# A gated mix of memory attention and a ReGLU block: an earlier half of wk, a split first K, and a new written-out order

## The chip, the cores and the metric

The kernel runs on one core of a Trainium2 chip. The metric is device time in microseconds (us) of one execution; the time of a kernel is the median of its runs. Engines are named as the profile names them: PE is the matrix engine (PEld its weight loads), DVE the vector engine, ACT the scalar engine, POOL the GpSimd engine, and SP the engine that issues nearly all DMAs (SPq is its queue).

## The reference

The input x has 2048 tokens of 512 numbers, in bfloat16. Two branches read it, and a gate per token mixes them:

```
g = sigmoid(sum(x * gate_w))            # one number per token
a = attention(x, wq, wk, wv, beta) @ wo # 32 heads of 16, 4 segments of 512 tokens
b = (relu(x @ W_gate) * (x @ W_up)) @ W_down    # 1792 wide
out = g * a + (1 - g) * b
```

Within a segment s the attention is

```
p     = softmax(q k^T * scale + causal mask);  a_dot = p @ v
a_mem = phi(q) @ M / (phi(q) @ z + 1e-6)       # memory of the earlier segments
o     = sigmoid(beta) * a_mem + (1 - sigmoid(beta)) * a_dot
M += phi(k)^T @ v;  z += sum(phi(k))           # phi(t) = t + 1 if t > 0, else exp(t)
```

## The kernel before, in words

**Tiling.** The 512 input columns are four chunks of 128 (the contraction), and the 512 columns of Q and K four blocks of 128, eight heads each. A unit is one block of one segment; there are 16. The transposed input of a segment is `xT`, 128 x 4 x 512. Q and K come out transposed, each block in one PSUM bank, summed over the four chunks (L478, a full 128 x 128 matmul of 512 columns). DVE copies Q into `QT` (L569) and K into `ktr` (L585), then writes it three times into `KT` (L588) with every second head zeroed by `mcol_e` or `mcol_o`, so that one matmul of 32 rows serves one head.

**A score visit** (L636, and L649 for the diagonal pieces) is a group of row-tiled matmuls, four at a time side by side, that fills PSUM banks 0 to 3 with scores. ACT takes the exponential of all four banks in one instruction (L658) into one of six buffers `E`, or into `Em`. There are 72 visits: four for each unit and one more for every second unit. Because each visit uses banks 0 to 3, it must wait for the exponential of the visit before. POOL then clears what the causal mask forbids (L687, two instructions for each visit that goes to `E`); for `Em` DVE does it (L669).

**Output product.** `pv` (L709) multiplies E with V in two groups of column-tiled matmuls, each into a bank. DVE transposes both banks into `T` (L740), takes the reciprocal of the softmax sum (L748), multiplies it by `grc`, the gates (L750), scales (L745), and transposes back into `oT` (L721).

**Head gates.** sigmoid(beta) is computed once: ACT's exponential (L410), `head_gates` on DVE, then `row_gates` (L402, L404) spreads it into `gcat`, 20 copies on DVE, and `pair_gates` (L408) makes `bdg` of it. `grc` is the product of `gcat` and the token gate `rq`, which POOL spreads in segment 0 (L448).

**The wide block** has 14 column blocks: gate, ReLU on ACT (L873), up, product on DVE (L879) into one of 14 buffers `hT`. The output rows then sum over the 14 `hT` with `wd_sb` and over `oT` with `wo_sb`. All of these matmuls, the projections and the output rows are called flexible: they may be issued as one full matmul (L478) or as four quarters of 32 columns of weights (L482), which is the tiling of `pv`. Between two visits the matmuls form a stretch. In the kernel before, a flexible matmul is quartered if the column-tiled group `pv` stands before it in the stretch.

**What sets the order.** Every piece of work is a task of a `Plan`: an engine, a duration that the planner assumed, dependencies, and buffer slots. The planner itself is not in the file; its result is: `ORDER` lists the tasks in the order of issue, and `UNITS` the slot of each ring (which PSUM bank, which `hT`). Each engine runs its tasks in this order, and waits by semaphores where the data need it. `LANDS` are the arrival times that the planner assumed for the loads; they set nothing at run time.

**The loads at the start.** SP issues, in order: the first half of the columns of x for half of the tokens, chunk 0 of wq, the transposed second half of x (L304, chunks 2 and 3 of `xT`), chunks 2 and 3 of wq (L306), both halves of wk, wv, and the pieces of W_gate and W_up; ACT's queue issues the other half of x's first columns and chunk 1 of wq. Chunks 0 and 1 of `xT` are made by PE (L515: eight transposes) and copied by DVE and ACT (L530). Before that PE runs seven matmuls on constants (L924). In the order before, PE then does Q's chunks 0 and 1 for all four blocks, Q's chunks 2 and 3, K of three blocks, some of V, and the first score visit.

Of the kernel before, what the change touches and what calls it, by code (L numbers as in the profile page):

```python
# [12 lines left out]
P = 128  # L13
# [13 lines left out]
RQ = 5  # L27
RH = 14

ORDER = """  # L30
# [99 lines left out]
class Plan:  # L130

    def __init__(self):
        self.tasks, self.free = [], {}
# [9 lines left out]
    def add(self, *a, **k):  # L143
        t = Task(*a, **k)
        t.n = len(self.tasks)
        self.tasks.append(t)
        return t
# [32 lines left out]
def kernel(  # L180
# [492 lines left out]
    def attention(seg, c):  # L673
# [17 lines left out]
        if c % 2 == 0:  # L691
            diag(seg, c)
# [298 lines left out]
```

## Time and profile before

| what | before |
|---|---|
| median of 3 runs | 263.82 us (263.33 to 264.11) |
| span of the profiled execution | 261.6 us |
| its own time | not listed beside the span |
| PE busy | 254.8 us, 97% |
| DVE busy | 203.4 us, 78% |
| ACT busy | 183.3 us, 70% |
| POOL busy | 64.2 us, 25% |
| mean granted PE clock | 0.998 |

The span is the time from the first to the last instruction of the profiled execution; the 2.2 us up to the median lie around it. Busy times overlap between the engines. A PE row of the timeline gives its start and how long its matmuls were in flight; the ends are modelled and overlap the next row, so the pace of PE is read from the distance of two starts.

### The profile page before, as it was taken

Reading aid. Unit: us, or ns where it says so; the run is one execution under the profiler, and the core shown is the slowest. Engines: PE = TensorE matmul, PEld = TensorE weight load, DVE = VectorE, ACT = ScalarE, POOL = GpSimd, SP = SyncE. Lnnn points to the kernel's source line nnn. Section 1 sums busy time; section 2 is a strip of 40 time slices with the busy share of each in tenths; the row PEclk is TensorE's granted clock in tenths of the full one; section 3 lists DMA queues with packets and bytes.
Section 4 is the critical chain, followed back from the end, with each engine's and each line's share of the span. In section 5 each row is a group of like instructions: output and inputs, shape, how many; then the busy total and the mean of one; then the engine's idle time right before and its main releaser. Section 6 shows DMA issues by size and latency. Waiting matters only on the chain.

```text
span 261.6 us, 8758 instructions
## 1 busy us (share of the span) xinstructions
PE 254.8 (97%) x3769; PEld 117.2 (45%) x3798; DVE 203.4 (78%) x472; ACT 183.3 (70%) x168; POOL 64.2 (25%) x168
## 2 busy tenths in 40 slices
PE   8999999999999999999999999999999999999995
PEld 3444444454444454544444444445444344445454
DVE  2799999889896766948989868858988678788622
ACT  3199998998877788787768576878486768972000
POOL 8023462313322223322112222122122232120000
PEclk9999999999999999999999999999999999999999
DMA  7999885021311202100210500140200100230011
GB/s 193 305 289 283 214 262 109 4 43 23 84 34 43 89 25 80 36 0 3 84 21 3 95 4 26 58 142 3 80 4 23 32 5 23 98 107 3 3 43 40
DMA packets 31565, 19.71 MB, mean 75 GB/s; under 512 B 16040, under 2 KB 29992, under 8 KB 31528
## 3 DMA queue, kind: packets, MB, share of 16 engines
q1 hardware_dynamic: 31112, 18.90, 26.3%
q8 instruction: 29, 0.48, 0.8%
q10 hardware_dynamic: 416, 0.26, 0.3%
q14 instruction: 8, 0.07, 0.1%
HBM read 13.21 MB, written 2.55 MB: 60 GB/s over the span
## 4 chain that ended last, share of the span: by engine, by line
PE 90%; DVE 5%; DMA 1%; issue 1%; SPq 1%; ACT 0%; DVEq 0%; ACTq 0%
PE ps L478 54%; PE ps L482 19%; PE ps L636 8%; PE ps L709 7%; DMA wq_sb<-in_A_wq_dram 1%; PE ps L649 1%; DVE ktr L585 1%; DVE KT L588 1%; PE ps L829 1%; SPq L304 1%; DVE QT L569 0%; PE ps L765 0%; DVE T L740 0%; DVE hT L879 0%; PE ps L805 0%
## 5 line engine op out<-in xcount | busy, mean ns | idle before, releaser
L658 ACT ACTIVATE E<-ps 128x2048 bf16<-128x2048 f32 x64 | 120.1, 1877 | 32.0 <-PE ps L636 21.8
L687 POOL TENSOR_SCALAR_AFFINE_SELECT E<-E 128x256 bf16<-128x256 bf16 x128 | 55.6, 458 | 170.0 <-ACT E L658 169.9
L879 DVE TENSOR_TENSOR hT<-ps,rgr 128x512 bf16<-128x512 f32 x56 | 37.8, 684 | 13.1 <-PE ps L478 8.4
L478 PE MATMUL ps<-xT,wu_sb 128*128 128x512 bf16 x163 | 45.6, 380 | 0.7 <-issue 0.5
L873 ACT ACTIVATE rgr<-ps 128x512 bf16<-128x512 f32 x56 | 32.6, 596 | 15.3 <-PE ps L482 8.2
L478 PE MATMUL ps<-wd_sb,hT 128*128 128x512 bf16 (+1 forms) x174 | 41.7, 354 | 0.6 <-issue 0.5
L478 PE MATMUL ps<-xT,wg_sb 128*128 128x512 bf16 x149 | 40.9, 380 | 0.3
L740 DVE STREAM_TRANSPOSE T<-ps 128x512 f32<-128x512 f32 x32 | 22.2, 706 | 6.8 <-PE ps L709 6.6
L636 PE MATMUL ps<-QT,KT 32*128 32x320 bf16 (+3 forms) x512 | 25.4, 273 | 0.3
L478 PEld LDWEIGHTS <-wu_sb 128*128 128x128 bf16 x170 | 15.3, 98 | 19.4 <-issue 3.0
L478 PEld LDWEIGHTS <-hT 128*128 128x128 bf16 x178 | 15.6, 98 | 17.6 <-issue 2.1
L905 DVE TENSOR_SCALAR osr<-ps,ngcol 128x512 bf16<-128x512 f32 (+2 forms) x18 | 12.3, 691 | 13.3 <-PE ps L482 9.1
L478 PEld LDWEIGHTS <-wg_sb 128*128 128x128 bf16 x156 | 14.3, 98 | 17.8 <-issue 2.1
L709 PE MATMUL ps<-E,Vp 128*17 128x320 bf16 (+3 forms) x512 | 19.3, 273 | 0.0
L636 PEld LDWEIGHTS <-KT 32*128 32x128 bf16 x512 | 7.6, 92 | 25.7 <-issue 24.6
L658 ACT ACTIVATE Em<-ps 128x2048 bf16<-128x2048 f32 x8 | 15.0, 1874 | 5.0 <-PE ps L649 5.0
L482 PE MATMUL ps<-xT,wg_sb 128*32 128x512 bf16 x272 | 17.8, 379 | 0.0
L482 PE MATMUL ps<-wd_sb,hT 128*32 128x512 bf16 (+1 forms) x296 | 16.9, 359 | 0.0
L478 PE MATMUL ps<-wv_sb,xT 128*128 128x512 bf16 x59 | 16.7, 380 | 0.2
L478 PE MATMUL ps<-xT,wq_sb 128*128 128x512 bf16 x57 | 15.9, 382 | 0.5 <-DMA wq_sb<-in_A_wq_dram 0.4
L478 PE MATMUL ps<-xT,wk_sb 128*128 128x512 bf16 x54 | 15.3, 379 | 0.2 <-issue 0.2
L482 PE MATMUL ps<-xT,wu_sb 128*32 128x512 bf16 x216 | 15.0, 379 | 0.0
(100 smaller groups left out, 293.7 us busy)
## 6 DMA issues: line engine op xcount, KB each, us to landing
out_dram<-osr SPq DMA_DIRECT2D x15, 128.0 KB
wd_sb<-in_B_W_down_dram SPq DMA_DIRECT2D x2, 896.0 KB
xn<-in_A_x_dram SPq DMA_DIRECT2D x3, 512.0 KB
cdr<-coefs SPq DMA_DIRECT2D x6, 256.0 KB
xn<-coefs SPq DMA_DIRECT2D x6, 256.0 KB
wg_sb<-in_B_W_gate_dram SPq DMA_DIRECT2D x2, 512.0 KB
wu_sb<-in_B_W_up_dram SPq DMA_DIRECT2D x2, 512.0 KB
wg_sb<-in_B_W_gate_dram SPq DMA_DIRECT2D x2, 384.0 KB
```

The lines of the kernel that those rows point to most:

```text
L304: nc.sync.dma_start_transpose(out=xT[0][:, NC // 2:NC, :], in_=x[0:L, halves[1]])
L478: nc.tensor.matmul(out, lhsT=lhsT, rhs=rhs, start=start, stop=stop)
L482: nc.tensor.matmul(out[r], lhsT=lhsT[:, r], rhs=rhs, start=start, stop=stop, tile_position=(0, 32 * j))
L585: d = plan.add("DVE", 600, key - RQK, lambda: nc.vector.tensor_copy(ktr[ks.i][:], bank(sl)), [a], DVL + 40, need=[ks], frees=[sl])
L636: nc.tensor.matmul(ps[:, j * L + o:j * L + o + L - q], lhsT=KT[i][rows, kb, 3 * r:3 * r + 2].rearrange("p h q -> p (h q)"), rhs=QT[i][rows ...
L658: last_exp[0] = [plan.add("ACT", 66 + 4 * L / 1.2, key, lambda: nc.scalar.activation(dst, ps[:, 0:4 * L], ACT.Exp, scale=SCALE), [a] + war ...
L687: nc.gpsimd.affine_select(out=m[:, :, o:o + HP], in_=m[:, :, o:o + HP], compare_op=ALU.is_ge, fill=0.0, base=HP, pattern=[[0, 4], [1, HP]] ...
L709: nc.tensor.matmul(bank(sl)[32 * m:32 * m + HW, q:q + w], lhsT=(Vp[i] if n < 4 else Vm)[:, kb, r, 4 * c + j, 0:HW], rhs=rhs, start=(n == 0 ...
L740: done.append(plan.add("DVE", 633, key - RL, lambda r=r, sl=sl: nc.vector.transpose(T[ts.i][:, r], bank(sl)), [a] + done, 75 if r else 0, ...
L873: r = plan.add("ACT", 478, key - RL, lambda sl=gsl, rs=rs: nc.scalar.activation(rgr[rs.i][:], bank(sl), ACT.Relu), [g], ACL, frees=[gsl])
L879: nc.vector.tensor_tensor(hT[hs1.i][:], bank(sl), rgr[rs.i][:], ALU.mult)),
L905: nc.vector.tensor_scalar(osr[os.i][:, n0 - c0:n1 - c0], bank(sl)[:, 0:n1 - n0], ngcol[:, tt:tt + 1], None, ALU.mult)),
```

## The change

The diff carries several changes together.

1. **Loads.** The first half of wk (chunks 0 and 1) is issued right after chunk 0 of wq, then chunks 2 and 3 of wq, and only then the transposed half of x. The second half of wk follows, and from there on the queue is as before.
2. **A new `ORDER` and new `UNITS`.** At the start PE does six matmuls of Q's chunks 0 and 1, then chunks 0 and 1 of K for all four blocks, and then the rest of Q and K mixed. Everything after that is ordered anew too, on every engine and in SP's queue.
3. **Quarters.** A stretch that holds any column-tiled group is quartered as a whole, also ahead of that group (`settle`). 65 matmuls that were full become quartered.
4. **Head gates.** The 20 copies of `row_gates` run on POOL instead of DVE.
5. **Buffers.** `KT` has four buffers instead of five (`RK`), `ktr` four instead of three. The overwriting of `QT` and `KT` now waits for the score visits that read them, instead of for the output product of the old unit, and that of `pqT` for the recall and the denominators.
6. **Recall** (the product with the memory M) is two tasks of two blocks instead of one of four.
7. **Visits** are built by one function from a list of items (`tape`); with the values at the end (`SIZES`, `BANKS`, `CUT`) a visit holds the same matmuls in the same order as before, and one exponential. `tag` is a label only.

```
-    LANDS = dict(n0=3470, n1=3600, q0=4500, q1=4550, x0=5600, q2=5900, q3=6400, ka=7700,
-                 kb=9600, v=11000, ...
+    LANDS = dict(n0=3470, n1=3600, q0=4500, q1=4550, ka=5500, q2=6600, q3=6600, x0=7700,
+                 kb=8900, v=11000, ...
...
     got_q = [load_wq(nc.sync, 0), load_wq(nc.scalar, 1)]
+    got_k = [load_rows(nc.sync, wk_sb, A_wk, 0, "k")]
+    nc.sync.dma_start(out=wq_sb[:, 2:NC, :],
+                      in_=A_wq.rearrange("(c p) n -> p c n", p=P)[:, 2:NC, :])
     nc.sync.dma_start_transpose(out=xT[0][:, NC // 2:NC, :], in_=x[0:L, halves[1]])
     got_x0b = arrival("x0")
-    nc.sync.dma_start(out=wq_sb[:, 2:NC, :],
-                      in_=A_wq.rearrange("(c p) n -> p c n", p=P)[:, 2:NC, :])
     got_q += [arrival("q%d" % ci) for ci in range(2, NC)]
-    got_k = [load_rows(nc.sync, wk_sb, A_wk, i, "k") for i in range(2)]
+    got_k.append(load_rows(nc.sync, wk_sb, A_wk, 1, "k"))
...
     def row_gates(m):
-        nc.vector.tensor_copy(gcat[rows, 1], g[rows, 1, :, m])
+        nc.gpsimd.tensor_copy(gcat[rows, 1], g[rows, 1, :, m])
         for c in range(NC):
-            nc.vector.tensor_copy(gcat[rows, 0, c], g[rows, 0, c, (m + c) % 4])
+            nc.gpsimd.tensor_copy(gcat[rows, 0, c], g[rows, 0, c, (m + c) % 4])
...
+        def settle():
+            col = any(t.mode == "col" for t in stretch)
+            for t in stretch:
+                t.col = bool(t.flex) and col
+            stretch.clear()
...
             if t.eng == "PE":
-                t.col = bool(t.flex) and mode == "col"
-                mode = mode if t.col else t.mode
+                if t.mode in ("row", "quad"):
+                    settle()
+                else:
+                    stretch.append(t)
...
-    KT = [sb([P, 4, 5, P // 2], BF16, f"KT{i}") for i in range(RQ)]
+    KT = [sb([P, 4, 5, P // 2], BF16, f"KT{i}") for i in range(RK)]
-    ktr = ring([P, L], BF16, "ktr", 3)
+    ktr = ring([P, L], BF16, "ktr", 4)
...
-        war = [att.get(("pv", u - RQ)), att.get(("recall", u - RQ))]
+        old = u - RK
+        war = [att.get(("score", old)), att.get(("score", old // 2 * 2, "d"))]
...
+        for half in range(2):
+            cs = (2 * half, 2 * half + 1)
+
+            def pe(cs=cs):
+                for c in cs:
+                    for j, m in turned(c):
...
+    CUT = 4
+    SIZES = [4] * 72
+    BANKS = [range(4)] * 72
```

More of the change, by code (lines that the diff above doesn't have):

```diff
@@ L132, in __init__ @@
     def __init__(self):
-        self.tasks, self.free = [], {}
+        self.tasks, self.free, self.tag = [], {}, ""
     def pool(self, name, n):
@@ L565, in proj_q @@
         else:
-            a = matmuls(key, list(got_q) + war, sl, proj_mm(wq_sb, c, seg),
+            a = matmuls(key, list(got_q) + [(w, 0.25) for w in war if w], sl, proj_mm(wq_sb, c, seg),
                         chunk={ci: got_x[seg][ci // 2] for ci in range(NC)})
@@ L569, in proj_q @@
         prj["q", seg, c] = plan.add("DVE", 600, key - RQK, lambda: nc.vector.tensor_copy(
[L570 removed]
+            QT[i][:], bank(sl)), [a] + war, DVL, frees=[sl])
         if seg:
@@ L654, in score @@
[L654 to L671 removed]
+    eread, exps = {}, {}
@@ new lines, in item @@
+    def item(u, f, j):
+        rows = slice(32 * j, 32 * j + 32)
+        if f == "d":
+            for v in range(2):
+                i = (u + v) % RQ
+                for kb in range(4):
+                    yield (KT[(u + v) % RK][rows, kb, 2:4], QT[i][rows, kb * P:kb * P + HP],
+                           4 * HP * v + HP * kb, HP)
+        else:
+            i, r = u % RQ, f % 2
+            for kb, q, o in PIECES[f // 2]:
+                yield KT[u % RK][rows, kb, 3 * r:3 * r + 2], QT[i][rows, q:L], o, L - q
@@ new lines, in target, with visit, pe @@
+    def target(u, f, j0, j1):
+        if f == "d":
+            return Em[:, j0:j1].rearrange("p j v k q -> p (j v k q)")
+        return E[(NFILL * u + f) % RE][:, j0 * L:j1 * L]
+    def visit(items, key, banks):
+        mm, busy = [], [0.0] * 4
+        for n, (u, f, j) in enumerate(items):
+            for lhsT, rhs, o, w in item(u, f, j):
+                mm.append((busy[j], j, n, lhsT, rhs, banks[n] * L + o, w))
+                busy[j] += w + 6
+        mm.sort(key=lambda m: m[:3])
+        def pe():
+            for _, j, _, lhsT, rhs, o, w in mm:
+                nc.tensor.matmul(ps[:, o:o + w], lhsT=lhsT.rearrange("p h q -> p (h q)"), rhs=rhs,
+                                 start=True, stop=True, tile_position=(32 * j, 0))
+        runs = []
+        for n, (u, f, j) in enumerate(items):
+            if (runs and runs[-1][1:3] == [u, f] and runs[-1][4] == j and n - runs[-1][0] < CUT
+                    and banks[n] == banks[n - 1] + 1):
+                runs[-1][4:6] = j + 1, n + 1
+            else:
+                runs.append([n, u, f, j, j + 1, n + 1])
+        sls = [Slot([tuple(("ps", b) for b in banks[n0:n1])]) for n0, _, _, _, _, n1 in runs]
+        deps = []
+        for u, f in dict.fromkeys(it[:2] for it in items):
+            for w in ((u, u + 1) if f == "d" else (u,)):
+                deps += [prj["q", w // 4, w % 4]] + prj["k", w // 4, w % 4]
+        a = plan.add("PE", max(busy) / 2.4 + 17, key - QKP, pe, deps, 275, mode="row", need=sls, size=16)
+        for (n0, u, f, j0, j1, n1), sl in zip(runs, sls):
+            if f == "d":
+                att["score", u, "d"] = a
+                wars = [att[k] for k in (("pv", u - 1), ("pv", u - 2)) if k in att]
+            else:
+                wars = eread.get(NFILL * u + f - RE, [])
+                att["score", u] = a
+            rd = max(sum(w + 6 for _, _, _, w in item(u, f, j1 - 1)) * (1 + (n1 > 4)), 0) / 2.4 + 17
+            exps.setdefault((u, f), []).append(plan.add(
+                "ACT", 66 + (n1 - n0) * L / 1.2, key,
+                lambda n0=n0, n1=n1, u=u, f=f, j0=j0, j1=j1: nc.scalar.activation(
+                    target(u, f, j0, j1), ps[:, banks[n0] * L:(banks[n0] + n1 - n0) * L], ACT.Exp,
+                    scale=SCALE), [(a, 275 - max(0.0, max(busy) / 2.4 + 17 - rd))] + wars, ACL, frees=[sl]))
@@ L787, in recall @@
     def recall(seg):
+        plan.tag = "recall"
         i, sls = seg % 2, [work() for _ in range(NC)]
@@ L799, in recall @@
                 .to_broadcast([8, 16, L])), [att["coefs", seg, c // 2]] + war, 4200, xfer=1850.0))
-        def pe():
-            for c in range(NC):
-                for j, m in turned(c):
-                    rows = slice(32 * j, 32 * j + 32)
-                    nc.tensor.matmul(bank(sls[c])[32 * m:32 * m + 32],
-                                     lhsT=mbd[i][rows, c].rearrange("p r e -> p (r e)"),
-                                     rhs=pqT[units[c] % RQ][rows, :], start=True, stop=True,
-                                     tile_position=(32 * j, 32 * m))
@@ L809, in recall @@
[L809 to L818 removed]
+        for half in range(2):
[3 more added lines that the diff above has]
+                    for j, m in turned(c):
+                        rows = slice(32 * j, 32 * j + 32)
+                        nc.tensor.matmul(bank(sls[c])[32 * m:32 * m + 32],
+                                         lhsT=mbd[i][rows, c].rearrange("p r e -> p (r e)"),
+                                         rhs=pqT[units[c] % RQ][rows, :], start=True, stop=True,
+                                         tile_position=(32 * j, 32 * m))
+            a = plan.add("PE", 240, key + half, pe, [prj["pq", seg, c] for c in cs]
+                         + [att["mbd", seg - 1]] + [(loads[c], 3900.25) for c in cs], PEL,
+                         need=[sls[c] for c in cs], mode="quad", size=8)
+            for c in cs:
+                om = plan.one("omr")
+                att["recall", units[c]] = a
+                att["omul", seg, c] = plan.add("DVE", 605, key - RL, lambda c=c, om=om: (
+                    nc.vector.tensor_tensor(omr[om.i][:], bank(sls[c]), coef[c], ALU.mult)),
+                    [a, loads[c]], DVL, need=[om], frees=[sls[c]])
+                recalled[units[c]] = att["omul", seg, c], om
@@ L912, in out_tile, with FILLS, score @@
             1400 if tt == NT - 1 else 2400, frees=[os], xfer=400.0)
+    def FILLS(u):
+        return [0, 1, 2, 3] + ["d"] * (u % 2 == 0)
+    tape = [(u, f, j) for u in range(4 * NSEG) for f in FILLS(u) for j in range(4)]
+    tape_done, seen = set(), [0, 0]
+    def score():
+        v, n = seen
+        items = tape[n:n + SIZES[v]]
+        seen[:] = v + 1, n + len(items)
+        visit(items, KA(items[0][0] - LEAD, AUNIT * (n % 18) / 18), BANKS[v])
+        tape_done.update(it[:2] for it in items if it[2] == 3)
+    CUT = 4
+    SIZES = [4] * 72
+    BANKS = [range(4)] * 72
     OTW, OBANKS, MEMGAP = 3, (7, 6), 1600.25
```

116 lines of the change are left out of this document (42 added, 74 removed), and 125 rows, old and new, of the table ORDER.

## The prediction

> **What bounds the kernel now.** I read the page's engine totals first, then the engines by stage, then the PE rows in order of time. The totals:
>
> ```profile
> PE 254.8 (97%) x3769; PEld 117.2 (45%) x3798; DVE 203.4 (78%) x472; ACT 183.3 (70%) x168; POOL 64.2 (25%) x168
> ```
>
> TensorE (PE) works 254.8 of 261.6 us, so the other 6.8 us are all there is to win unless the matmuls change. The view by stage (each row: the stretch, its length, busy time of PE, PEld, DVE, ACT, POOL, granted clock, DMA share, GB/s) says where they lie:
>
> ```profile
> 0.00:3.46 3.46, 2.62 (x7) 0.89 (x8) 0.51 (x7) 1.28 (x1) 2.61 (x10) 1.00 0.39 122
> 3.46:4.55 1.09, 1.09 (x11) 0.93 (x10) 0.63 (x2) 0.37 (x1) 1.09 (x4) 1.00 1.15 271
> 4.55:6.53 1.98, 1.98 (x9) 0.71 (x8) 0.22 (x1) 0.37 (x1) 1.75 (x12) 1.00 1.00 271
> 6.53:6.89 0.36, 0.00 (x1) 0.01 (x1) 0.00 (x0) 0.00 (x0) 0.00 (x0) 1.00 1.07 307
> 6.89:12.61 5.72, 5.57 (x27) 2.45 (x29) 4.54 (x10) 1.23 (x2) 0.00 (x0) 1.00 0.97 310
> 12.61:232.50 219.89, 217.37 (x3198) 97.68 (x3226) 182.25 (x427) 175.36 (x158) 57.61 (x142) 1.00 0.27 71
> 232.50:258.71 26.21, 26.21 (x524) 14.51 (x522) 14.87 (x27) 4.68 (x7) 1.17 (x4) 1.00 0.10 33
> 258.71:261.60 2.89, 0.00 (x0) 0.00 (x0) 0.35 (x1) 0.00 (x0) 0.00 (x0) 0.85 0.08 23
> ```
>
> Outside the warm-up (0.84 idle) and the last output (2.89), PE is idle 0.36 us in one piece at 6.53, and 2.52 us spread over the 220 us that hold the score visits. The PE rows tell what the 2.52 are. A score visit is the group of row-tiled matmuls at L636 or L649:
>
> ```profile
> 12.61 0.40 PE L636 MATMUL ps<-QT,KT 32*128 32x448 bf16 x8
> 15.20 0.40 PE L636 MATMUL ps<-QT,KT 32*128 32x448 bf16 x8
> 18.23 0.40 PE L636 MATMUL ps<-QT,KT 32*128 32x320 bf16 x8
> 23.32 0.59 PE L478 MATMUL ps<-xT,wg_sb 128*128 128x512 bf16 x2
> 23.75 0.59 PE L478 MATMUL ps<-xT,wu_sb 128*128 128x512 bf16 x2
> 29.48 0.40 PE L636 MATMUL ps<-QT,KT 32*128 32x448 bf16 x8
> 32.32 0.40 PE L636 MATMUL ps<-QT,KT 32*128 32x320 bf16 x8
> 42.84 0.60 PE L482 MATMUL ps<-xT,wu_sb 128*32 128x512 bf16 x8
> 43.27 1.04 PE L482 MATMUL ps<-xT,wk_sb 128*32 128x512 bf16 x16
> ```
>
> Two full matmuls take 23.75-23.32 = 0.43 us, 0.216 each; eight quarter matmuls (column tiles, two full ones' work) also 0.43. From 12.61 to 15.20 the program puts one visit and 10 full matmuls: 2.59 = 10 x 0.216 + 0.43. From 15.20 to 18.23, one visit and 12: 3.03 = 12 x 0.216 + 0.43. So a visit costs a fixed 0.43, its two changes of tiling included, and no wait is left beside it. From 29.48 to 32.32 stand 11 full matmuls' worth of column-tiled columns: 2.84, 0.03 above the formula. PE is a dense stream, and the time is its work plus its waits.
>
> **The change part by part.** The profiled execution's own time is not listed beside its span. I sum against the span of 261.6 and carry the difference to the median of the three runs, 263.82 - 261.6 = 2.2, unchanged.
>
> *Work on PE.* In program order both kernels have 72 visits and 151 changes of tiling, and the same columns. 65 full matmuls become 260 quarters: 65 x (0.216 - 4 x 0.054) = 0. Three more stretches are column-tiled: 3 x 0.03 = +0.1. The memory recall becomes two tasks, but its 16 matmuls still follow each other: 0. Before the first visit stand 40 projection matmuls in place of 34: 6 x 0.216 = 1.3 us moved, not added.
>
> *The loads.* This is the front, with the queue that issues (SPq) and PE:
>
> ```profile
> 1.82 1.31 SPq L304 DMA_TRANSPOSE xT<-in_A_x_dram  x1
> 3.19 0.57 SPq L306 DMA_DIRECT2D wq_sb<-in_A_wq_dram  x1
> 3.81 0.97 SPq L267 DMA_DIRECT2D wk_sb<-in_A_wk_dram  x2
> 4.13 0.80 ACT L530 CAST xT<-ps 128x256 bf16<-128x256 f32 x2 [0.98 <-PE ps L515]
> 4.55 1.97 PE L478 MATMUL ps<-xT,wq_sb 128*128 128x512 bf16 x8
> 6.89 1.90 PE L478 MATMUL ps<-xT,wq_sb 128*128 128x512 bf16 x8 [0.36 <-DMA wq_sb<-in_A_wq_dram]
> 8.62 2.75 PE L478 MATMUL ps<-xT,wk_sb 128*128 128x512 bf16 x12
> ```
>
> PE runs out of Q's first two chunks and waits 0.36 us for the rest of wq. In the new order six of Q's matmuls, eight of K's (chunks 0 and 1, all four column blocks) and one more of Q come before anything needs the transposed half of x or the rest of wq: needed at 4.55 + 15 x 0.216 = 7.79. Is it there? By 6.89 the rows by stage moved 122 x 3.46 + 271 x 3.07 + 307 x 0.36 = 1.36 MB, where what PE waited for ends at 1.05 MB of the issue order (four loads of 131 KB, two of 262): up to 0.31 MB of later loads ran beside it. A load that ends at B MB then lands between the moments when B and B + 0.31 MB have moved. First half of wk (now 0.79 MB): 4.8 to 6.0, needed at 4.55 + 6 x 0.216 = 5.85. Transposed half (1.31 MB): 6.7 to 7.7, needed at 7.79. Second half of wk (1.57 MB, as before): 7.6 to 8.6, needed at 4.55 + 20 x 0.216 = 8.87, where before the same place first used it at 8.62 + 6 x 0.216 = 9.92. All come out just in time. The lower end of the cost is 0; the upper is 9.92 - 8.87 = 1.05, since the trace proves only that the second half of wk was there by 9.92. I take 0.1, near the byte counts: the term is -0.36 + 0.1 = -0.26. Q's chunk 1 is now used by the third matmul, at 4.98, and ACT's copy of it ends at 4.13 + 0.80 = 4.93: 0.
>
> On the SP queue the transposed half moves back past two issues, 0.49 + 0.57 plus gaps, about 1.1 us; from the second half of wk on, every issue keeps its place. The K halves hold eight PSUM banks together with Q's, but no eviction by DVE stands before Q's end, and its chain to the first visit has 4 us.
>
> *Shorter stretches.* The new order has 25 stretches of ten full matmuls, before had 3. In such a one ACT must finish an exponential within 2.59 us:
>
> ```profile
> 13.06 1.88 ACT L658 ACTIVATE E<-ps 128x2048 bf16<-128x2048 f32 x1 [0.55 <-PE ps L636]
> 14.83 0.59 ACT L873 ACTIVATE rgr<-ps 128x512 bf16<-128x512 f32 x1
> 15.31 0.63 ACT L548 ACTIVATE ex<-ktr 128x512 bf16<-128x512 bf16 x1
> ```
>
> The exponential starts 0.45 after its visit (13.06 - 12.61) and gives the queue on after 1.77; the visit at 15.20 was not late, 2.14 after that start: 0.45 + 2.14 = 2.59 fits exactly. With one small operation (0.48, 15.31-14.83) ACT needs 2.25, with two 2.77, 0.18 too much, which a neighbouring stretch without one absorbs. Lower end 0, upper end 4 pairs x 0.18 = 0.7; I take 0, as the 2.59 row shows no wait. KT has four buffers instead of five, ktr four instead of three: a K projection's copies now wait for the score visits of four units before, which come earlier than the output products they waited for: 0, or one eviction of DVE (0.6) if I have the order wrong.
>
> *The head gates.* Twenty small copies move from DVE to POOL:
>
> ```profile
> L404 DVE COPY gcat<-gall 32x2 f32<-32x2 f32 x16 | 1.7, 167 | 0.0
> L402 DVE COPY gcat<-gall 32x8 f32<-32x8 f32 x4 | 0.8, 194 | 0.1
> 20.62 1.33 POOL L687 TENSOR_SCALAR_AFFINE_SELECT E<-E 128x256 bf16<-128x256 bf16 x2 [1.89 <-ACT E L658]
> 23.64 0.80 POOL L687 TENSOR_SCALAR_AFFINE_SELECT E<-E 128x256 bf16<-128x256 bf16 x2 [1.69 <-ACT E L658]
> 30.13 3.75 POOL L448 COPY rq<-rcol 32x4 f32<-32x4 f32 x16
> 37.80 1.45 POOL L687 TENSOR_SCALAR_AFFINE_SELECT E<-E 128x256 bf16<-128x256 bf16 x2 [2.25 <-ACT E L658]
> 20.91 0.77 DVE L432 SCALAR_TENSOR_TENSOR junk<-xn,gwb 128x512 bf16<-128x512 bf16 x1
> 30.91 0.23 DVE L408 TENSOR_SCALAR bdg<-gcat,mcol_e 128x4 f32<-128x4 f32 x1
> 32.13 1.30 DVE L740 STREAM_TRANSPOSE T<-ps 128x512 f32<-128x512 f32 x2
> 37.93 0.68 DVE L745 TENSOR_TENSOR och<-T,cfr 128x512 bf16<-128x512 f32 x1
> ```
>
> DVE loses 1.7 + 0.8 = 2.5 us, off the path, so no gain. POOL gains 20 x 3.75/16 = 4.7. The new wait is DVE's: the two operations that read gcat (L408, now L419) stand in its queue right ahead of the transposes that empty the first output product's two banks. In the new order (first visit at 4.55 + 40 x 0.216 + 0.1 = 13.3, then 3.03, 2.59, 3.03) the fourth exponential ends at 21.95 + 0.45 + 1.88 = 24.3. Then POOL has three masks, 8 copies for rq and 10 of gcat before DVE may go: 3 x 0.80 + 18 x 0.234 = 6.6 at least, 3 x 1.45 + 4.2 = 8.6 at most: 30.9 to 32.9. The transposes could start at 31.7 by PE, and PE asks for the first bank back 0.4 us after they would have freed it, so POOL may run to about 31.8 free of cost. Cost 0 to 1.1; the mean of the pairs shown (0.80, 1.33, 1.45) gives 24.3 + 3.6 + 4.2 = 32.1, 0.3 late. I take 0.2.
>
> The two long pairs stand beside DVE operations whose two inputs both lie in SBUF (20.91, 37.93). [...]
>
> *The sum.* +0.1 - 0.26 + 0 + 0.2 = +0.04; the span goes to 261.6 and the time to 263.9. The diff's other lines (tags, one list of visits) issue nothing.
>
> **The rivals.** (1) Slower: the second half of wk lands no earlier than its old use proves. PE then stands still up to 1.05 us at 8.87: 263.82 + 0.1 - 0.36 + 1.05 + 0.2 = 264.8. For it: 310 GB/s is all that the front moves, and PE now wants it 1.05 us sooner. Against it: the byte count says 8.6. It decides from a landing after 9.6. (2) Slower by POOL's queue: 3 x 1.45 for the masks and DVE waits for gcat: 263.82 + 0.1 - 0.26 + 1.1 = 264.8, from a POOL end after 32.6. (3) The wait only changes its name: PE waits for the transposed half, which by a fixed delay from issue (landed by 6.89, issued at 1.82; now about 2.95) comes by 8.0: 8.0 - 7.79 = 0.2 in place of 0.36; 264.0, no change. (4) Faster: the 0.36 goes and a third of the 2.52 us between visits with it: 263.82 - 0.36 - 0.84 = 262.6. Against it: the number of visits and changes is the same. (5) The quarters pay for their weights. Rows:
>
> ```profile
> L478 PEld LDWEIGHTS <-wg_sb 128*128 128x128 bf16 x156 | 14.3, 98 | 17.8 <-issue 2.1
> L482 PEld LDWEIGHTS <-wg_sb 128*32 128x32 bf16 x272 | 6.6, 97 | 5.2
> ```
>
> A quarter's load takes 97 ns, a whole one's 98; exposed, 65 x (4 x 97 - 98) = 18.9 us: 282.7. Against it: 42.84 to 43.27 shows the quarters at full pace. [...]
>
> **How the numbers follow.** No change 0.52 and rival 3 0.13: 0.65 within 0.3% (0.8 us, about what a measurement of this kernel can tell from no change). Rival 1 0.12, rival 2 0.11, rival 5 0.01, small waits of the new order together (one eviction of 0.6 more than once) 0.03: 0.27 slower. Rival 4 0.08 faster. The likeliest: 263.9, its own range 263.4 to 264.5. The range takes in rivals 1 to 3 and their half way together: 263.2 to 265.2.
>
> **What would show it.** The 0.36 before L490's matmuls for the rest of wq gone, at most 0.1 for wk or xT instead; the first visit near 13.3; stretches of 2.59 with no wait between 13 and 232; PE busy within 0.3 us of 254.8; DVE's L419 without a wait on POOL. A wait of PE on wk before 9.9, or of DVE on gcat near 31 with PE waiting for T's bank, would make it wrong on the slow side.

## The result, and the profile after

The changed kernel takes 265.10 us (median of 4 runs, 264.48 to 265.51) against 263.82 (263.33 to 264.11): a ratio of 1.0049, 95% interval 1.0029 to 1.0068. It is slower by half a per cent, where the prediction's likeliest case was no change; the time lies inside its range, which had been widened for rivals of which, as shown below, none came. The profiled run took 264.48 us for a span of 262.8, so 1.7 us lie around a span. One of the runs before is 263.33 = 261.6 + 1.7: the profiled run before was probably its fastest, and the 2.2 carried in the prediction too much by half a microsecond.

The page of the changed kernel, engine totals and the chain that ended last:

```profile
PE 255.8 (97%) x3965; PEld 119.1 (45%) x3993; DVE 202.2 (77%) x452; ACT 182.9 (70%) x168; POOL 68.0 (26%) x188
PE 97%; issue 1%; DVE 0%
```

The chain is now PE nearly without a break, and 1% of it (2.6 us) is "issue": time in which PE waited for nothing that the profile shows. Both profiles lack some 28 matmul records (3965 of 3993 here), so PE's busy time can't be compared to tenths of a microsecond. The starts of single rows can. The front, as rows of PE (start, time in flight):

```profile
4.57 2.07 PE L490 MATMUL ps<-xT,wq_sb 128*128 128x512 bf16 x6
6.47 1.89 PE L490 MATMUL ps<-xT,wk_sb 128*128 128x512 bf16 x8
8.20 0.38 PE L490 MATMUL ps<-xT,wq_sb 128*128 128x512 bf16 x1
13.91 0.40 PE L681 MATMUL ps<-QT,KT 32*128 32x448 bf16 x8
```

No matmul here waits for a load; the 0.36 is gone. But the first visit comes at 13.91, 1.30 later than before, which is just the six matmuls moved ahead of it: nothing was won in this run, because the first six matmuls took 6.47 - 4.57 = 1.90 us where six at the later pace take 1.30. From first to last visit before took 220.07 us (12.61 to 232.68) and after 219.91 (13.91 to 233.82), with 1.30 us less to do: 1.14 us have come in. Most of them stand in one place, rows of PE, of its weight loads, and of SP's queue:

```profile
110.79 0.40 PE L681 MATMUL ps<-QT,KT 32*128 32x320 bf16 x8
111.18 0.66 PE L875 MATMUL ps<-Vp,pK 128*32 128x34 bf16 x64
111.67 1.06 PE L494 MATMUL ps<-xT,wq_sb 128*32 128x512 bf16 x16
112.53 0.61 PE L494 MATMUL ps<-xT,wk_sb 128*32 128x512 bf16 x7
113.43 0.40 PE L494 MATMUL ps<-xT,wk_sb 128*32 128x512 bf16 x4 [0.29 <-issue]
113.44 0.12 PEld L494 LDWEIGHTS <-wk_sb 128*32 128x32 bf16 x7 [0.78 <-issue]
108.67 0.61 SPq L839 DMA_DIRECT2D xn<-coefs  x1
109.39 3.27 SPq L284 DMA_TRANSPOSE xT<-in_A_x_dram  x1
```

In the middle of sixteen quarters on one tile, with the same operands before and behind, PE stops. Its weight loads stand still from 112.56 to 113.44 us, 0.88 where their pace is 0.21, so 0.67 is lost. The program has no wait there. So the prediction's picture (work plus waits on data) had no name for what cost most. In the trace's DMA records a single packet of 16 KB on a queue of kind "instruction" started at 111.07 us. There are 31 such packets on that queue for about 8,000 PE instructions (3,993 loads, as many matmuls), one for each 258. The suspicion: PE had run out of instructions.

### The profile page after: what moved, and what is told of

Same layout as the page of the kernel before. It is cut to its first block, busy times and chain, and to the rows that moved or that the text cites. A ratio compares the mean times of both kernels' runs of the same rounds, so it can differ in the third digit from the quotient of the medians.

```text
span 262.8 us, 9105 instructions
## 1 busy us (share of the span) xinstructions
PE 255.8 (97%) x3965; PEld 119.1 (45%) x3993; DVE 202.2 (77%) x452; ACT 182.9 (70%) x168; POOL 68.0 (26%) x188
## 4 chain that ended last, share of the span: by engine, by line
PE 97%; issue 1%; DVE 0%
PE ps L490 53%; PE ps L494 26%; PE ps L681 9%; PE ps L749 7%; PE ps L988 1%; PE ps L875 1%; PE ps L850 0%; PE ps L528 0%; PE ps L806 0%; DVE osr L953 0%; PE ps L537 0%
## 5 line engine op out<-in xcount | busy, mean ns | idle before, releaser
L722 POOL TENSOR_SCALAR_AFFINE_SELECT E<-E 128x256 bf16<-128x256 bf16 x128 | 53.6, 452 | 165.7 <-ACT E L706 160.2
L490 PE MATMUL ps<-xT,wu_sb 128*128 128x512 bf16 x154 | 42.4, 380 | 0.5 <-issue 0.3
L681 PE MATMUL ps<-QT,KT 32*128 32x64 bf16 (+3 forms) x768 | 28.7, 245 | 0.0
L494 PE MATMUL ps<-wd_sb,hT 128*32 128x512 bf16 (+1 forms) x476 | 28.5, 367 | 0.0
L490 PE MATMUL ps<-wd_sb,hT 128*128 128x512 bf16 (+1 forms) x126 | 27.1, 344 | 0.8 <-issue 0.8
L681 PEld LDWEIGHTS <-KT 32*128 32x128 bf16 x768 | 9.9, 92 | 26.9 <-issue 25.9
L494 PE MATMUL ps<-xT,wu_sb 128*32 128x512 bf16 x248 | 17.3, 380 | 0.0
L490 PEld LDWEIGHTS <-hT 128*128 128x128 bf16 x133 | 11.1, 98 | 12.0 <-issue 1.9
L494 PEld LDWEIGHTS <-hT 128*32 128x32 bf16 x476 | 11.7, 97 | 9.7 <-issue 1.1
L585 DVE CAST QT<-ps 128x512 bf16<-128x512 f32 x16 | 10.8, 682 | 6.5 <-PE ps L490 5.9
```

Of the source, the lines that this page charges most:

```text
L490: nc.tensor.matmul(out, lhsT=lhsT, rhs=rhs, start=start, stop=stop)
L494: nc.tensor.matmul(out[r], lhsT=lhsT[:, r], rhs=rhs, start=start, stop=stop, tile_position=(0, 32 * j))
L585: prj["q", seg, c] = plan.add("DVE", 600, key - RQK, lambda: nc.vector.tensor_copy(QT[i][:], bank(sl)), [a] + war, DVL, frees=[sl])
L681: nc.tensor.matmul(ps[:, o:o + w], lhsT=lhsT.rearrange("p h q -> p (h q)"), rhs=rhs, start=True, stop=True, tile_position=(32 * j, 0))
L722: nc.gpsimd.affine_select(out=m[:, :, o:o + HP], in_=m[:, :, o:o + HP], compare_op=ALU.is_ge, fill=0.0, base=HP, pattern=[[0, 4], [1, HP]] ...
```

## The experiments

The median of the kernel before, run beside each group, was 263.7, 263.8 and 263.9 us. In the diffs, the stretches are numbered in program order; `FULL` names those in which only what stands behind a column-tiled group is quartered (the rule before), `QUART` those that are quartered although they hold none. Both change the number of PE's instructions and not its work.

**A second profile.**

> The changed kernel once more, nothing altered, for a second profile. Two places of the first one are in question. (a) The first six Q matmuls, which took 1.90 us there (weight loads 0.42 us apart until 5.8 us) against 1.30 at the later pace: if the slow pace is a draw of the run, the second profile starts the full pace at some other time between 4.4 and 6.5 us and the first scoring visit moves with it, anywhere from 13.3 to 13.95 us; if it belongs to the new loads it is again at 13.9. (b) The 0.67 us in which PE stood at 112.6 to 113.4 us with no wait of the program on it. Theory F: PE had run out of instructions; 16 KB of them had been asked for at 111.07 us, and PE issued the next 176 loads and matmuls within 1.5 us, the shortest such time in the trace (the next shortest took 2.3 us and had no gap). Theory D: a late operand or a chance stall. F expects a gap of 0.5 to 0.8 us at the same two instructions; D as chance expects none. Time 264.5 to 265.5.

265.62 us, just above the forecast, span 263.9. The gap is at the same two instructions, 113.05 to 113.99. A second one stands in the memory update of the next segment:

```profile
192.04 0.55 PE L875 MATMUL ps<-Vp,pK 128*32 128x34 bf16 x50
193.10 0.27 PE L875 MATMUL ps<-Vp,pK 128*32 128x34 bf16 x14 [0.51 <-issue]
```

The first six Q matmuls took 2.41 us this time and the first visit came at 14.40, later than the 13.95 allowed for a draw. So the stop belongs to the program, and the slow start is a draw all the same, as the later profiles confirm (13.35 to 14.40); this one was the worst.

**Shifting the count of instructions.**

```
-            col = any(t.mode == "col" for t in stretch)
+            col = any(t.mode == "col" for t in stretch) or nth[0] in QUART
+            seen = nth[0] not in FULL
             for t in stretch:
-                t.col = bool(t.flex) and col
+                seen = seen or t.mode == "col"
+                t.col = bool(t.flex) and col and seen
+            nth[0] += 1
# less24: FULL = (7,)    more60: QUART = (8,)    before_more144: two stretches of twelve
```

> The changed kernel with one early stretch (the one with the first product of E and V, near 30 us) quartered only behind that product: two tasks of two full matmuls each stay full, so PE's program is 24 instructions shorter from there on, its work the same. Theory F: each 256-instruction fetch now stands 24 instructions further on in the work, so the fetch near 111 us starts at the memory update rather than at the visit ahead of it, PE needs about 2.3 us for the next 176 instructions in place of 1.5, and the gap of 0.67 us falls to about 0.1; everywhere else the time for 176 instructions stays at 2.3 us or more. Time about 0.5 us below the changed kernel's 265.1, so 264.4 to 264.8. Theory D: the gap stays at 0.67 us behind the visit near 110.8, the time at 265.0 to 265.2.

> The changed kernel with one more early stretch of ten full matmuls quartered (near 35 us), 60 more instructions for PE and the same work; the quarters themselves cost nothing by both theories (0 to 0.1 us). Theory F: the fetch near 111 us starts 60 instructions earlier in the work, PE needs 1.28 us for the 176 behind it, and the gap grows from 0.67 to about 1.1 us and moves into the memory update itself (near 111.6 us in place of 112.6). Time 0.4 us above the changed kernel's, about 265.5. Theory D: gap of 0.67 us at the same instruction as before, time 265.0 to 265.3.

> The kernel before, with two of its early stretches of twelve full matmuls quartered (near 28 to 38 us): 144 more PE instructions, the same work. In the profile of before no stretch of 176 instructions behind a fetch takes under 2.3 us and PE has no gap without a wait. Theory F: shifted by 144 instructions, three fetches fall ahead of dense places, near 53.8 us (1.74 us for the 176), 104.8 us (1.67) and 178.5 us (2.16), which leaves gaps of about 0.6, 0.7 and 0.2 us: time 1.3 to 1.6 us above before, near 265.3, slower by as much as the whole change was, without any of its parts. Theory D: the quarters cost 0 to 0.1 us, so 263.8 to 263.9 and no gaps.

All three forecasts of the time by theory F failed, and theory D's for the first two as well. less24: 266.04 us (ratio 1.0086, 1.0066 to 1.0106), worse. more60: 264.42 (1.0020, 1.0008 to 1.0032), better than the changed kernel. before_more144: 263.79 (1.0004, 0.9993 to 1.0014), unchanged, though its profiled run, the slowest of twelve at 264.61, does have a gap of 0.89 at 181.8 us. The gaps themselves told what was wrong with F. Rows of the weight loads in less24 and in more60:

```profile
113.56 0.10 PEld L686 LDWEIGHTS <-KT 32*128 32x128 bf16 x4 [0.42 <-issue]
115.18 0.10 PEld L686 LDWEIGHTS <-KT 32*128 32x128 bf16 x4 [1.52 <-issue]
```

```profile
110.57 0.57 PEld L880 LDWEIGHTS <-pK 128*32 128x32 bf16 x58 [0.21 <-issue]
112.26 0.11 PEld L880 LDWEIGHTS <-pK 128*32 128x32 bf16 x6 [1.12 <-issue]
```

The work at the gap differs (a visit in one, the memory update in the other), but counted in weight loads it is the same place. All gaps of this kind in the profiles of these runs and of the next group, from the trace's DMA records and weight loads (us; "behind load" counts the weight loads ahead of the gap, the last column is from the landing to PE's next load):

```
kernel               behind load  packet   took  landed   PE stops  resumes  behind
after                    1630     111.07   1.03  112.10    112.56   113.44    1.34
after_again              1630     111.56   1.09  112.65    113.05   113.99    1.34
after_less24             1630     112.90   1.02  113.92    113.57   115.18    1.26
after_more60             1630     109.26   0.96  110.22    111.05   112.26    2.04
after_xt66               1630     110.70   0.95  111.65    112.07   112.87    1.22
after_xt66               2782     189.46   0.89  190.35    191.29   191.76    1.40
after_again              2782     189.41   2.22  191.63    192.41   193.10    1.47
after_less60             2782     191.08   0.95  192.03    192.47   193.40    1.37
after_less60_xt66        2782     190.84   0.98  191.82    192.37   193.27    1.45
before_more144            733      54.80   0.92   55.72     57.00    57.24    1.52
before_more144           2653     180.29   0.93  181.22    181.76   182.65    1.43
before_xt103             1501     108.18   1.10  109.28    108.41   110.72    1.44
```

2782 - 1630 = 9 x 128, and the others lie within one load of multiples of 128 from there: the gaps stand whole multiples of 256 instructions apart (128 loads and their matmuls), wherever the work is, and with one packet for each 258 I take these places for the boundaries of blocks of 256. In eleven of twelve cases PE goes on 1.2 to 1.5 us after the packet landed, and at none of the boundaries in the fourteen profiles does it take up a block sooner than 1.2 us after that. What my first theory had wrong was the packet's start: it isn't at a fixed count, but anywhere from 2.5 us before PE enters the block ahead to 3.9 us after. less24 lost more since its packet started 2.5 us after. more60 isn't explained by its gap: its stretch is 1.18 us longer than without a gap, and yet its median is 0.7 us below the changed kernel's. Its profiled run (264.41 us) had a front 0.56 us earlier than the changed kernel's; what its other runs had was not seen. That gave the second theory, F2, a supposition: a block must come while PE passes the one ahead of it, and that fails where PE passes 256 instructions quickly (2.46 us in the changed kernel) and data traffic delays the packet (it started there 0.98 us after PE had entered the block ahead).

**Traffic, and blocks that last longer.** The order moved the transposed load of the fourth segment from 64 us, in the kernel before, to 109.

```
# xt66: the load's entry in ORDER placed near 66 us      (1015 behind 44)
# less60: FULL = (7, 11, 15)                              less60_xt66: both
# before_xt103: the same load placed near 103 us          (1013 behind 350)
```

> The changed kernel with one load moved: the transposed load of the fourth segment of x is issued near 66 us, about where the kernel before had it (64.1), and not at 109.4. PE's program is untouched. Theory F2, after the gaps of the first runs: PE's instructions come in blocks of 256, each asked for when PE enters the block ahead of it; a gap lies at the same count of instructions whatever is shifted, and ends 1.3 to 1.5 us after the block's packet has landed. At that place PE goes through the block ahead in 2.46 us, and the packet started 0.98 us (changed kernel) or 2.5 us (less24) after the request, because the many small packets of the transposed load lie ahead of it. Without that load the delay is 0.3 to 0.6 us, as elsewhere; the packet takes 1.0: the block is there 2.7 to 3.1 us after the request, and the gap is 0.2 to 0.6 us in place of 0.9. Time 0.5 to 0.9 us below the changed kernel's 265.2: 264.3 to 264.7. Rival D2, the density of instructions alone, no traffic: gap 0.9 as before, time 265.2.

> The changed kernel with three early stretches (those with the first products of E and V and the first memory update) quartered only behind a product: PE's program is 60 instructions shorter from 54 us on, its work the same, the transposed load still at 109.4 us. By F2 the block ahead of the former gap now starts 60 instructions further on, in the middle of the memory update, and PE needs 4.6 us for it; no block of the program is left under 4.0 us. With the transposed load still in the way (delay up to 2.5, packet 1.0, 1.3 to 1.5 behind it) the next block is there 4.8 us after the request at the worst: gap 0 to 0.3 us. Time 264.0 to 264.5 against 265.2. D2 (density alone) expects the same here. If the gap belonged to the memory update and its quarters whatever the count, it stays and the time is 265.2.

> Both of the former: 60 instructions fewer ahead of the place, and the transposed load near 66 us. By F2 no gap anywhere: the shortest block takes 4.0 us against 3.1 at the most for its successor. Time 263.9 to 264.4, what is left of the change once its stall is taken out: the first visit 0.2 to 0.4 us earlier for the same work than before, against the slower recall and memory stretches (0.4 to 0.5 us). If it is under 263.7 it beats both kernels.

> The kernel before with one load moved: the same transposed load is issued near 102.8 us in place of 64.1, nothing else. PE's program is untouched. Its tightest block there is the one entered at 105.2 us: PE takes 2.94 us for it, and its successor was asked for, started 0.5 us later and landed at 106.6, with 0.16 us to spare by F2 (landing and 1.35 us against 108.12). With the transposed load's packets under way from 103.5 us on, F2 expects a delay of 1 to 2.5 us and a gap of 0.3 to 2.0 us at the instruction that PE starts at 108.1 us: time 264.0 to 265.7, median about 264.6. D2 (density alone): no gap, 263.7.

before_xt103 is the plainest: one load moved in the kernel before, PE's program untouched, and 267.58 us (1.0122, 1.0089 to 1.0154), 3.8 slower, far more than the forecast 264.0 to 265.7. Its rows, PE and SP's queue:

```profile
107.89 0.40 PE L635 MATMUL ps<-QT,KT 32*128 32x448 bf16 x8
108.21 0.53 PE L708 MATMUL ps<-E,Vp 128*17 128x448 bf16 x10
110.72 0.31 PE L708 MATMUL ps<-E,Vp 128*17 128x320 bf16 x4 [1.99 <-issue]
111.06 2.97 PE L481 MATMUL ps<-xT,wg_sb 128*32 128x512 bf16 x30
103.14 3.78 SPq L273 DMA_TRANSPOSE xT<-in_A_x_dram  x1
```

and the same place in the kernel before, without a stop:

```profile
107.59 0.40 PE L636 MATMUL ps<-QT,KT 32*128 32x448 bf16 x8
107.92 0.61 PE L709 MATMUL ps<-E,Vp 128*17 128x448 bf16 x16
108.36 0.29 PE L709 MATMUL ps<-Em,Vm 128*17 128x64 bf16 x16
108.48 1.90 PE L482 MATMUL ps<-xT,wg_sb 128*32 128x512 bf16 x32
```

The transposed load's packets of about 256 bytes ran from 105.0 to 108.25 us, over a thousand a microsecond at the end, and the instruction packet started at 108.18, 2.7 us after PE had entered its block; before it started 0.5 after, landed at 106.61 and was used at 108.12. It had come 1.51 us ahead, which by the table is just enough: by its lags the kernel before was itself within 0.3 us of this stall, an estimate.

The gap is 2.3 us of the 3.8. The rest stands behind it: the quarters from 111.06 take 2.97 us for 30, where before 32 take 1.90, since the granted clock reads 0.50 from 111.72 to 115.13 us (1.00 before and after that). Half pace for 3.41 us loses 1.7, an estimate. Four of the six runs have a mean granted clock of 0.993 or 0.994 and take 267.52 to 268.14 us; the two at 1.00 take 265.55 and 265.97, what the gap alone costs. In no other profile here, with gaps of 1.6 us and less, does the granted clock fall between the first visit and the last. That the long stop brings the low clock is the likely reading, and not shown: one run of six of smooth_old_loads (below) has a mean of 0.994 and the long time too, 267.58 us, and no stop of this kind stands in that kernel's profile.

In the changed kernel the transposed load is not the main culprit. after_xt66, without it, took 264.64 us (1.0038, 1.0025 to 1.0052), 0.46 less by the medians and 0.3 by the ratios, whose intervals overlap. Its gap is 0.80 where I expected 0.2 to 0.6, and a second one stands at load 2782. At the first the packet still started 1.1 us late, with the packets of the `coefs` reads (L839) under way from 109.5 us. after_less60 took 264.49 (1.0023, 1.0009 to 1.0037), at the upper end of what was expected, and less60_xt66 264.47 (1.0020, 1.0007 to 1.0033), above it: in both the gap near 112 is gone, and one of 0.9 stands at load 2782, where the packet starts 2.4 to 2.6 us after PE has entered the block ahead, and the load of `xn` for the last segment was issued at 187.6. The block ahead lasts 4.0 us in them, which I had called enough; in less60 the packet's delay, its transfer and the time behind the landing come to 2.57 + 0.95 + 1.38 = 4.9.

**Without gaps; and parts of the change undone.**

```
# smooth: FULL = (7, 11, 15), QUART = (46, 50), load near 66 us
# gates_dve: smooth, row_gates on nc.vector again, as in the kernel before
# old_loads: smooth, transposed half of x and rest of wq ahead of the first half of wk
# old_rule: the changed kernel, every stretch as FULL
```

> The changed kernel, its blocks of 256 PE instructions shifted in two steps so that none of them is passed quickly: three early stretches quartered only behind a product (60 instructions fewer from 54 us on), two stretches of ten full matmuls between the third and fourth segments quartered (120 more from 140 us on), and the transposed load near 66 us as in after_xt66. Work and order are the same. F2: the shortest block then takes 4.2 us (in the changed kernel 2.47 and 3.8), and no successor needs over 3.8 us from request to use (the latest seen: 2.43 to 2.57 us of delay, 1.0 of transfer, 0.4 behind it to the last instruction already there): no gap at 112 us and none at 192, where the former two runs had 0.9. Time 263.8, from 263.5 to 264.2: what the change does without its instruction stalls, and the same as before. If the gaps were not what costs, 264.4 as the former two.

> after_smooth with the copies of row_gates back on DVE, as before the change; 20 small copies leave POOL's queue and enter DVE's. PE's program is untouched. If POOL's copies held the masks or DVE's pair_gates up, this is 0.2 to 1.1 us faster than after_smooth; if DVE's time counts there (20 copies of some 0.1 us in front of the stage of the first products), it is up to 0.5 slower. The trace of the changed kernel shows DVE's pair_gates without a wait, so I expect the same time within 0.2 us.

> after_smooth with the early loads in the former order: the transposed half of x, the rest of wq, then both halves of wk; the order of the matmuls stays as changed. The eight K matmuls come up at 5.9 to 6.7 us and need the first half of wk, which by this order lands about 0.9 us after the rest of wq (6.9 us in the trace of before): PE waits 1.1 to 1.9 us at the K matmuls, and not again, since all that follows has landed by then. Time 1.1 to 1.7 us above after_smooth, 264.9 to 265.5. If the loads are hidden anyway, the same time as after_smooth.

> The changed kernel with the former rule for quarters throughout (only what stands behind a product or memory update is quartered), the transposed load at 109.4 us as in the changed kernel. PE has some 190 matmuls and as many weight loads fewer, for the same work. Theory F2, by count: the boundaries fall so that the 256 instructions entered at 109.8 us (products, visit and memory update) are passed in 1.9 us, faster than in the changed kernel (2.47), so the gap is there again and larger, 1.2 to 2.5 us, though the program is shorter: time 265.3 to 266.5. Rival Q: the stall comes of the instructions that quartering adds. Then there is no gap here, and the time is 264.0 to 264.3.

**after_smooth** took 263.81 us (ratio to before 0.9997, 0.9985 to 1.0008), as forecast. From less60_xt66 it differs by 120 PE instructions for the same work, and it is 0.66 us faster. The same place as above:

```profile
111.27 0.66 PE L880 MATMUL ps<-Vp,pK 128*32 128x34 bf16 x64
111.76 1.05 PE L499 MATMUL ps<-xT,wq_sb 128*32 128x512 bf16 x16
112.63 1.05 PE L499 MATMUL ps<-xT,wk_sb 128*32 128x512 bf16 x16
113.61 0.40 PE L686 MATMUL ps<-QT,KT 32*128 32x320 bf16 x8
```

Sixteen quarters from 112.63, the visit 0.98 later, no stop; the trace has no other stop of this kind either, and at every boundary the block had landed at least 2.8 us before PE came to it.

**Gates back on DVE** took 264.56 us (1.0028, 1.0017 to 1.0039), 0.75 above smooth; I had expected no difference. Compared visit by visit, two stretches are longer, by 0.48 and 0.36 us. Rows of PE and of DVE:

```profile
27.19 0.59 PE L495 MATMUL ps<-xT,wg_sb 128*128 128x512 bf16 x2 [0.33 <-DVE Vp L639]
31.96 0.37 PE L754 MATMUL ps<-E,Vp 128*17 128x448 bf16 x4 [0.28 <-DVE hT L931]
25.43 0.39 DVE L418 COPY gcat<-gall 32x8 f32<-32x8 f32 x1
25.73 0.82 DVE L420 COPY gcat<-gall 32x2 f32<-32x2 f32 x4
26.46 0.67 DVE L639 CAST Vp<-ps 128x512 bf16<-128x512 f32 x1
```

Five small copies stand ahead of the copy that empties V's bank, and PE waits for the bank; ten more, from 30.18 us, stand ahead of the hT product that the second row waits for.

**Old loads**: 265.59 us (1.0077, 1.0050 to 1.0103), 1.8 above smooth, a little over the forecast. The first visit comes at 15.27, in place of 13.70, and from there to the last visit nothing differs:

```profile
7.83 1.04 PE L495 MATMUL ps<-xT,wk_sb 128*128 128x512 bf16 x4 [1.02 <-DMA wk_sb<-in_A_wk_dram]
```

**Old rule**: 266.11 us (1.0084, 1.0059 to 1.0109). The time falls in F2's range, and for the wrong reason: there is no gap. The packet left at 110.39, ahead of the first packets of the reads (111.0), landed at 111.37 and was used at 112.97. What costs is the tiling: 15 stretches are each 0.09 to 0.12 us longer than in smooth, 1.5 us together, in stretches that go from full matmuls to a column-tiled group (20 such changes in the program, 3 in smooth, none in the changed kernel or in the kernel before). One of them, in old rule and in smooth:

```profile
81.80 0.40 PE L682 MATMUL ps<-QT,KT 32*128 32x448 bf16 x8
82.13 0.82 PE L491 MATMUL ps<-wd_sb,hT 128*128 128x512 bf16 x3
82.88 0.61 PE L750 MATMUL ps<-E,Vp 128*17 128x448 bf16 x16
84.84 0.39 PE L682 MATMUL ps<-QT,KT 32*128 32x320 bf16 x7
```

```profile
81.13 0.40 PE L686 MATMUL ps<-QT,KT 32*128 32x448 bf16 x8
81.46 0.83 PE L499 MATMUL ps<-wd_sb,hT 128*32 128x512 bf16 x12
82.12 0.61 PE L754 MATMUL ps<-E,Vp 128*17 128x448 bf16 x16
84.07 0.32 PE L686 MATMUL ps<-QT,KT 32*128 32x320 bf16 x4
```

From the three full matmuls to the product it takes 0.75 us, from the twelve quarters 0.66, for the same columns. Of the 2.4 us between the two profiled spans, 0.57 more is a later first visit and 0.30 lies behind the last one.

## Why the prediction was right or wrong, step by step

**"PE is a dense stream, and the time is its work plus its waits."** Right for the stretches: nearly all follow the formula within 0.06 us, the 25 short ones among them. Wrong in what a wait can be. This is the step that failed: the sum had no term for PE's own instructions. The changed order puts products, a visit, a memory update and 32 quarters close together, and PE passes one block of 256 instructions in 2.46 us; the quickest in the kernel before took 2.94. That the time still fell into the range is luck: the range was widened for rivals 1 to 3, and what came was none of them. In the profiled run the gap makes its stretch 0.66 us longer than in smooth, in the second profile two gaps cost 0.72 and 0.65. Smooth shows that the loss goes with them: the same work in the same order on PE, no gaps, and no difference left from before. How large the gaps were in the runs without a profile was not seen.

**"From the second half of wk on, every issue keeps its place."** Wrong, as a statement on SP's queue beyond the front: the transposed load of the fourth segment went from 64 to 109 us, next to the quick block. Moved alone, to a quick block of the kernel before, that load cost 3.8 us, low clock included. In the changed kernel it accounts for 0.3 to 0.5 of the 1.3 at most, not clear of the noise.

**Loads, -0.26.** It fits, though the draw of the start is larger than the term. In ten profiles with the changed front the first visit came at 13.35 to 14.40, mean 13.84; less the 1.30 of moved work that is 12.54. In three with the front of before it came at 12.61, 12.87 and 13.14, mean 12.87: -0.33, give or take some 0.2 by the scatter of these profiles. The wait that was to go is itself a draw: in the three the weight loads waited 0.8, 1.9 and 0.7 us in all for wq. In these ten no wait for xT's half or the second half of wk appears, so rivals 1 and 3 are out; for the first half of wk the weight loads waited 0.2 to 0.5 us in three of them, at the upper end of its byte count (6.0). The single profile didn't show it, since the first matmuls run at half pace for a time that varies:

```profile
4.57 1.46 PE L495 MATMUL ps<-xT,wq_sb 128*128 128x512 bf16 x6
5.91 1.90 PE L495 MATMUL ps<-xT,wk_sb 128*128 128x512 bf16 x8
```

These are the same six matmuls in more60: 1.34 us, against 1.90 and 2.41 above. The granted clock reads 1.00 in each. The full pace (0.21 us between loads in place of 0.42) began anywhere between 4.5 and 6.7 us. What decides that moment is not shown; over these profiles it spreads by about 2 us.

**Quarters, 0 and +0.1.** Right in effect: nothing measurable is lost by them, and before_more144, with 24 more full matmuls quartered, has the time of before. But the value of the new rule was missed. In the new order, under the old rule, a change from full to quarter within a stretch costs 0.10 us, 15 times between the first visit and the last; in the order before it didn't come up, because its products stand first in their stretches. So the new rule pays for what the new order would cost, and rival 5 (quarters that pay for their loads) is out.

**Head gates, +0.2.** The cost didn't come, and a gain that was put at nothing did. DVE's two operations on gcat start with no wait:

```profile
31.67 0.22 DVE L419 TENSOR_SCALAR bdg<-gcat,mcol_e 128x4 f32<-128x4 f32 x1
32.35 1.34 DVE L780 STREAM_TRANSPOSE T<-ps 128x512 f32<-128x512 f32 x2 [0.32 <-PE ps L749]
```

POOL was in time (rival 2 is out), and "DVE loses 2.5 us, off the path, so no gain" doesn't hold in the new order, where the copies on DVE cost 0.75. What they cost in the order before was not run.

**Shorter stretches and fewer buffers, 0.** Right for the short stretches, too small for the rest: by its work the recall's stretch near 120 us is 0.18 longer than the one before, the stretches with a memory update up to 0.1. From first to last visit, smooth without its three stretches held full takes 219.50 - 0.30 = 219.20 us, the kernel before 220.07 - 1.30 = 218.77 for the same work. These small terms, some 0.4 in all, eat what the front wins. Rival 4, faster, is out with them.

Of the signs that the prediction named, the first visit near 13.3 and PE's busy time near 254.8 were missed (13.91 and 255.8), 0.6 of each by the slow start; the wait of 0.36 was gone and DVE's L419 waited for nothing, as it said. So the sum of +0.04 described the change without its stalls (smooth: -0.1 to before), in part because a cost that didn't come and small terms that did offset each other, and the stalls were the 1.3 us that were missed.

## What to carry to other kernels

Where PE issues many small tiled matmuls, count its instructions in blocks of 256 (counted from the gaps here, the boundaries stand behind weight loads 94, 222, 350 and so on, give or take one): a block that PE passes in 4 us or less, with DMA traffic around it, is a place where PE can stop with no wait in the program (the stops here stand behind blocks of 2.2 to 4.0 us; not every such block brings one, and old rule passes one in 1.9 us without), and adding or removing a few instructions anywhere ahead moves that place. Look for it as "issue" idle of the weight loads in the middle of a uniform group, with an instruction packet landing 1.2 to 1.5 us before PE goes on. And compare the whole of the DMA queue's order, not only the part that the diff names: one load moved into such a place cost 3.8 us, about 2 by the stop and the rest by the low clock that followed.

A version that should beat both wasn't run: smooth pays three times 0.10 us for stretches held full only to shift the count. Shifted by added quarters in place of these, 0.3 less can be estimated, 263.5 us.

## What the runs showed of the hardware

There was one 16 KB instruction packet for each 258 of PE's loads and matmuls (31 for 7,986), and the gaps stand whole multiples of 256 instructions apart, give or take one load. A packet mostly took 0.9 to 1.4 us, at most 2.2, and started from 2.5 us before PE entered the block ahead to 3.9 us after; PE took up no block sooner than 1.2 us after its packet's landing. At 30 of the 31 boundaries in the profiled run no stop of this kind is seen; at the other one it costs 0.7 us, and at one in before_xt103 2.3. There, after PE had stood still for 2.0 us, the granted clock fell to 0.50 for 3.41 us. Why one kernel, more60, resumed only 2.0 us after the landing stays open, and so does what decides within a run when the packet starts.
